# A windowed softmax-weighted sum and a maxout layer on one core: part of the tap sums of columns 28 to 31 moved to VectorE, reductions in three parts, two products in two parts, and a test of the softmax sums with a second path

## Chip, cores and metric

The kernel runs on 1 core of one Trainium2 chip. The metric is the device time of one execution in microseconds. Engine names are TensorE (PE in the profile, PEld its weight loads), VectorE (DVE), ScalarE (ACT), GpSimd (POOL) and SyncE (SP).

## What is computed

```python
# x: (8, 4160, 192), weight_gen: (8, 4160, 8, 7)
w = np.exp(weight_gen - weight_gen.max(-1, keepdims=True))
w = w / (w.sum(-1, keepdims=True) + 1e-09)          # softmax over 7 taps, for each row and head
x_pad = zeros(6 rows) in front of x                  # in each of the 8 sequences
y[b, s, h*24:(h+1)*24] = sum over k of w[b, s, h, k] * x_pad[b, s + k, h*24:(h+1)*24]
h1, h2 = y @ w1, y @ w2                              # (33280, 192) @ (192, 1024)
out = np.maximum(h1, h2) @ w_out                     # (33280, 1024) @ (1024, 192)
```

The kernel uses max(h1, h2) = h1 + relu(h2 - h1): it multiplies y by the difference of the two weight matrices, takes the relu, multiplies by `w_out`, and adds y times the product of w1 and `w_out`. The softmax is taken without subtracting the maximum: exp, sum, logarithm, subtraction of the logarithm, exp.

## The kernel before

The 33280 rows are laid out as 128 partitions of 260 consecutive rows, called columns. A partition's columns are worked in 17 batches of 16 columns (the last has 4). A batch is cut into pieces, of 4 columns in batches 0 and 1 and of 8 after that. One piece is a unit: units 0 to 7 have 4 columns each, so unit 7 holds columns 28 to 31. Each unit has as many hidden tiles as columns; tiles are worked in groups of two up to tile 15 and of three from tile 16.

For a batch the steps are, by the functions that issue them: `exp_sum` (exp on ScalarE, L135), `red` (sum over the 7 taps on VectorE, L147), `ln` (logarithm on ScalarE, in place, L151), `shift` (subtraction on VectorE, L156), `weights` (exp on ScalarE, each value written twice, L167), `mul` (product of weights and x for all 7 taps on VectorE, L182), `adds` (three additions over the taps on VectorE, L198, L204 and L207), `transpose` (a DMA transpose that SyncE issues). `adds` lays other small steps between its additions by its argument `beside`: the `shift` of the next batch in three parts, or the `red` of a later batch in two.

Batches 0 and 1 differ: there `sum_transpose` lets TensorE add the taps and transpose, by matmuls with the identity (L248), and ScalarE copies the result out as `yt` (L255). With `adds(..., True)` VectorE first adds taps 3 to 5 onto taps 0 to 2, and TensorE then sums only the four that are left (`LEFT`); this is done for unit 5 alone.

The hidden layer of a tile is `hid_tile` (L299 on TensorE) and `relu` (L309 on ScalarE); the output is `out_first` and `out_second` (L351, L339 on TensorE), then `evac` (L395 on ScalarE, stores by SyncE, L409). The last four columns are stored by ScalarE and SyncE at L386.

The order is written out by hand and nothing is rescheduled (`manual_schedule`), so each engine works its instructions in the order of the program. In the opening the weights `w1` and `w2` are loaded in halves to `ws`, VectorE makes their differences `wd` (L584, L589), and ScalarE copies parts of them to other partitions (L586, L587, L591), so that TensorE can use pairs of half arrays. `keep_warm` gives TensorE matmuls without a use while it waits. GpSimd issues the loads of x and of `weight_gen`; `behind` makes such a load wait for an instruction of another engine. In the later groups a table (`AT`, with defaults) names the tile at which ScalarE gets `weights` (W), `ln` (l) or `exp_sum` (X) of a batch; in groups with four output columns a long step can be put off to the next group, unless the group's first tile is in `NOW`.

Of the kernel before, what the change touches and what calls it, by code (L numbers as in the profile page):

```python
# [23 lines left out]
def kernel(  # L24
# [20 lines left out]
    RPB = P // B  # L45
    G = D // H
# [29 lines left out]
    pwg = ctx.enter_context(tc.tile_pool(name="pwg", bufs=4))  # L76
    pxb = ctx.enter_context(tc.tile_pool(name="pxb", bufs=2))
    pe_ = ctx.enter_context(tc.tile_pool(name="pe", bufs=2))
    psm = ctx.enter_context(tc.tile_pool(name="psm", bufs=3))
    pm = ctx.enter_context(tc.tile_pool(name="pm", bufs=1))  # L80
    pen = ctx.enter_context(tc.tile_pool(name="pen", bufs=2))
    py = ctx.enter_context(tc.tile_pool(name="py", bufs=2))
    pyt = ctx.enter_context(tc.tile_pool(name="pyt", bufs=6))
    prd = ctx.enter_context(tc.tile_pool(name="prd", bufs=7))
    first_ps = ctx.enter_context(ExitStack())
# [3 lines left out]
    def later_ps():  # L89

        first_ps.close()
        for k in ("ab", "c", "r"):
            ps[k] = ctx.enter_context(tc.tile_pool(name="pps_" + k, bufs=1, space=bass.MemoryType.PSUM))
# [3 lines left out]
    wg_ts, xb_ts, e_ts, s_ts, en_ts, y_ts, yt_ts = {}, {}, {}, {}, {}, {}, {}  # L97
# [44 lines left out]

    def red(b, i=0, of=1):
        if i == 0:
            s_ts[b] = psm.tile([P, BATCHES[b][1] * H], FP32, name="sum_t", tag="sum")
        hs, at, ap = part(b, i, of)
        nc.vector.reduce_sum(out=s_ts[b][:, hs], in_=_sub(e_ts[b], at, ap), axis=AX.X)  # L147

    def ln(b, i=0, of=1):
        s_t = s_ts[b][:, part(b, i, of)[0]]  # L150
        nc.scalar.activation(out=s_t, in_=s_t, func=AF.Ln)  # L151

    def shift(b, i=0, of=1):
        hs, at, ap = part(b, i, of)
        w_t = _sub(wg_ts[b], at, ap)
        nc.vector.tensor_tensor(out=w_t, in0=w_t, in1=_sub(s_ts[b], hs.start, [[1, hs.stop - hs.start], [0, K]]),  # L156
                                op=ALU.subtract)

    def weights(b, o):
# [6 lines left out]
        for j in range(J):  # L166
            nc.scalar.activation(  # L167
                out=_sub(en_ts[b], (o * WGC + j * N * K) * 2, [[2 * N, K], [2, N], [1, 2]]),
                in_=_sub(wg_ts[b], (o * H + j * N) * K, [[1, K], [K, N], [0, 2]]), func=AF.Exp,
            )  # L170


    def mul(b, o):

        n = dict(pieces(b))[o]
        if n == 4 and b < 2:
            m_out = _sub(m_t, K * o * D, [[64, 2], [P, K * 6], [1, 64]])
            x_in = _sub(xb_ts[b], o * D, [[2 * D, 2], [D, K], [1, 2 * D]])
        else:
# [4 lines left out]
            in1=_sub(en_ts[b], o * WGC * 2, [[2, K * n * H], [0, G // 2], [1, 2]]),  # L184
# [54 lines left out]
    def sum_transpose(u, taps=range(K)):  # L239
# [3 lines left out]
        yps = ps["r" if "r" in ps else "o"].tile([P, 1024], FP32, name="yps", tag="op")  # L243
        for k in range(6):
            for t in taps:
                for r in range(2):
                    at = (K * o + t * n) * D + k * P
                    nc.tensor.matmul(  # L248
                        yps[:, r * 512 + k * 64:r * 512 + (k + 1) * 64],
                        lhsT=m_t[half(r), at:at + P], rhs=ident[half(r), half(r)],  # L250
                        start=(k == 0 and t == taps[0]), stop=(t == taps[-1]),
                        skip_group_check=True,
                    )
        yt = pyt.tile([P, 8 // 2 * 3 * P], BF16, name="yt", tag="yt")
# [122 lines left out]
    def evac(p, n):  # L377
# [20 lines left out]
        for q in range(p, p + n):  # L398
            u, i, _ = column(2 * q)
            if NU - 7 <= u < NU - 1 and i % 2:  # L400
                stores.append((nc.sync, place(q)[0] - 1, [4 * D, 2], [1, 2 * D]))
            elif u < NU - 7 and i == UNITS[u][2] // 2 - 1:
# [108 lines left out]
    gate = consts.tile([P, 1], FP32, name="gate")  # L511
    o_last = consts.tile([P, 2 * D], FP32, name="o_last")

    with tc.tile_pool(name="pstage", bufs=1) as pstage:
# [57 lines left out]
        for o in (0, 4, 8, 12):  # L572
            weights(0, o)
        nc.vector.tensor_copy(out=xb_ts[0][:, PAD * D:(PAD + 4) * D],
# [261 lines left out]
```

## Time and profile before

| | before |
|---|---|
| time, median of 3 runs | 409.5 us (409.34 to 410.65) |
| the profiled execution | 410.25 us, span 408.4 us |
| TensorE busy | 398.9 us (98%) |
| VectorE busy | 371.7 us (91%) |
| ScalarE busy | 357.1 us (87%) |
| GpSimd busy | 72.5 us (18%) |
| granted TensorE clock | 1.0 throughout |
| moved by DMA | 65.70 MB, mean 161 GB/s |

The span runs from the first instruction of the program to its last; the time of an execution has 1.85 us more around it. Times inside a profile are counted from the start of the span. A line such as "L182 DVE ... x37" is a group of instructions of one source line on one engine, and "idle before <- releaser" says how long the engine had nothing to do before them and what ended that.

### The profile page before, as it was taken

What the parts mean: (1) busy time and instruction counts of PE and PEld (TensorE: products, weight loads), DVE (VectorE), ACT (ScalarE), POOL (GpSimd) and SP (SyncE); (2) the same over time, 40 slices, a digit from 0 to 9 for tenths busy, and PEclk for the clock granted to TensorE, in tenths of its full rate; (3) what the DMA queues carried; (4) which work ended last, traced back from release to release, by engine and by line L of the source; (5) the groups of instructions that cost most, each with busy time, mean ns of one, the idle gap of its engine ahead of it and who ended that gap; (6) DMA issues with size and microseconds to landing.
All of it is one profiled execution on the core that took longest, in us unless ns stands there. A gap on an engine that the chain in (4) does not pass through costs nothing.

```text
span 408.4 us, 16153 instructions
## 1 busy us (share of the span) xinstructions
PE 398.9 (98%) x7422; PEld 317.6 (78%) x7422; DVE 371.7 (91%) x216; ACT 357.1 (87%) x424; POOL 72.5 (18%) x101
## 2 busy tenths in 40 slices
PE   7899999999999999999999999999999999999996
PEld 2589989777777777777877777777778777777796
DVE  4999999999999999999999999999999999999000
ACT  6799899999899998898998999998999988988872
POOL 0311012212222112121211122220122220210000
PEclk9999999999999999999999999999999999999999
DMA  8958399767658674976786588478648647654514
GB/s 242 218 125 219 75 186 167 168 165 173 147 113 237 151 167 105 244 201 69 234 203 84 123 248 202 65 243 180 128 109 239 169 68 237 154 127 111 145 55 142
DMA packets 62785, 65.70 MB, mean 161 GB/s; under 512 B 47711, under 2 KB 51679, under 8 KB 62718
## 3 DMA queue, kind: packets, MB, share of 16 engines
q1 hardware_dynamic: 54334, 40.54, 36.7%
q0 software_dynamic: 8240, 24.04, 29.9%
q8 instruction: 58, 0.95, 1.0%
q10 hardware_dynamic: 144, 0.10, 0.1%
q14 instruction: 9, 0.07, 0.1%
HBM read 35.96 MB, written 25.56 MB: 151 GB/s over the span
## 4 chain that ended last, share of the span: by engine, by line
PE 91%; ACT 4%; DMA 3%; issue 1%; SPq 0%; DVE 0%; ACTq 0%
PE op_ps L339 41%; PE hd L299 39%; PE op_ps L351 8%; DMA xs<-in_x_dram 3%; ACT rd_t L309 2%; PE hdp L299 1%; PE yps L248 1%; ACT yt L255 1%; ACT w1t L675 0%; ACT e_t L135 0%; ACT en_t L167 0%; DVE xb_t L620 0%; ACT wd L591 0%; ACT w L668 0%; ACT w1T L633 0%
## 5 line engine op out<-in xcount | busy, mean ns | idle before, releaser
L309 ACT ACTIVATE rd_t<-hd 128x1024 bf16<-128x1024 f32 (+1 forms) x206 | 234.7, 1187 | 27.5 <-PE hd L299 26.3
L339 PE MATMUL op_ps<-wo,rd_t 64*128 64x192 bf16 x4160 | 211.4, 243 | 0.1
L339 PEld LDWEIGHTS <-rd_t 64*128 64x128 bf16 x4160 | 181.7, 94 | 15.7 <-ACTq L372 0.3
L299 PE MATMUL hd<-yt,wd 64*128 64x512 bf16 (+1 forms) x1584 | 188.1, 360 | 0.7 <-issue 0.6
L182 DVE TENSOR_TENSOR m_t<-xb_t,en_t 128x10752 bf16<-128x10752 bf16 (+1 forms) x37 | 187.4, 5070 | 0.2
L299 PEld LDWEIGHTS <-wd 64*128 64x128 bf16 x1776 | 94.5, 94 | 43.2 <-issue 2.8
L224 POOL CAST gate<-yt 128x1 f32<-128x1 bf16 x29 | 37.8, 1305 | 264.3 <-DMA yt<-y_t 264.3
L198 DVE TENSOR_TENSOR m_t<-m_t 128x4608 bf16<-128x4608 bf16 (+1 forms) x30 | 74.1, 2470 | 0.1
L395 ACT COPY o_t<-op_ps 128x384 f32<-128x384 f32 (+1 forms) x99 | 57.3, 589 | 12.8 <-PE op_ps L339 12.8
L351 PE MATMUL op_ps<-w,yt 64*128 64x192 bf16 x780 | 56.0, 243 | 0.4 <-ACT w L668 0.4
L351 PEld LDWEIGHTS <-yt 64*128 64x128 bf16 x780 | 38.6, 94 | 16.7 <-issue 1.3
L204 DVE TENSOR_TENSOR m_t<-m_t 128x3072 bf16<-128x3072 bf16 (+1 forms) x29 | 50.0, 1723 | 0.1
L167 ACT ACTIVATE en_t<-wg_t 128x896 bf16<-128x896 f32 (+2 forms) x45 | 35.8, 821 | 0.0
L207 DVE TENSOR_TENSOR y_t<-m_t 128x1536 bf16<-128x1536 bf16 (+1 forms) x29 | 27.3, 941 | 0.5
L114 POOL DMA_DIRECT2D xb_t<-in_x_dram x33 | 17.6, 534 | 32.0 <-ACT rd_t L309 19.8
L147 DVE TENSOR_REDUCE sum_t<-e_t 128x64 f32<-128x448 f32 (+2 forms) x31 | 19.6, 635 | 3.3 <-ACT e_t L135 3.3
L156 DVE TENSOR_TENSOR wg_t<-wg_t,sum_t 128x280 f32<-128x280 f32 (+5 forms) x46 | 22.0, 481 | 0.0
L135 ACT ACTIVATE e_t<-wg_t 128x896 f32<-128x896 f32 (+2 forms) x18 | 16.1, 901 | 2.6 <-DMA wg_t<-in_weight_gen_dram 2.6
L309 ACT ACTIVATE rd_t<-hdp 128x1024 bf16<-128x1024 f32 x16 | 16.3, 1056 | 0.5 <-PE hdp L299 0.4
L299 PE MATMUL hdp<-yt,wd 64*128 64x256 bf16 x192 | 13.2, 270 | 0.7 <-issue 0.5
L615 PE MATMUL warm<-ident 128*128 128x512 bf16 x38 | 10.7, 449 | 2.6 <-DVE ident L562 2.6
L248 PEld LDWEIGHTS <-m_t 64*128 64x128 bf16 x636 | 10.1, 95 | 2.6 <-DVE m_t L182 2.5
(45 smaller groups left out, 65.9 us busy)
## 6 DMA issues: line engine op xcount, KB each, us to landing
out_dram<-o_t SPq DMA_DIRECT2D x22, 768.0 KB, 4.8
xb_t<-in_x_dram POOLq DMA_DIRECT2D x30, 384.0 KB, 5.2
out_dram<-o_t SPq DMA_DIRECT2D x20, 384.0 KB, 3.1
wg_t<-in_weight_gen_dram POOLq DMA_DIRECT2D x14, 448.0 KB, 5.3
xb_t<-xb_t POOLq DMA_DIRECT2D x16, 288.0 KB, 5.4
wg_t<-in_weight_gen_dram SPq DMA_DIRECT2D x2, 448.0 KB, 4.4
xs<-in_x_dram SPq DMA_DIRECT2D x2, 384.0 KB, 7.2
xb_t<-in_x_dram POOLq DMA_DIRECT2D x3, 192.0 KB, 4.4
```

Of the source, the lines that this page charges most:

```text
L156: nc.vector.tensor_tensor(out=w_t, in0=w_t, in1=_sub(s_ts[b], hs.start, [[1, hs.stop - hs.start], [0, K]]), op=ALU.subtract)
L167: nc.scalar.activation(out=_sub(en_ts[b], (o * WGC + j * N * K) * 2, [[2 * N, K], [2, N], [1, 2]]), in_=_sub(wg_ts[b], (o * H + j * N) * K ...
L182: return nc.vector.tensor_tensor(out=m_out, in0=x_in, in1=_sub(en_ts[b], o * WGC * 2, [[2, K * n * H], [0, G // 2], [1, 2]]), op=ALU.mult,)
L198: nc.vector.tensor_tensor(out=taps(0, 1, 3), in0=taps(0, 1, 3), in1=taps(3, 1, 3), op=ALU.add)
L204: nc.vector.tensor_tensor(out=taps(0, 2, 2), in0=taps(0, 2, 2), in1=taps(1, 5, 2), op=ALU.add)
L207: nc.vector.tensor_tensor(out=_sub(y_ts[b], o * D, [[64, 2], [P, 3 * w // 2], [1, 64]]), in0=taps(0, 1, 1), in1=taps(2, 1, 1), op=ALU.add,)
L224: nc.gpsimd.tensor_copy(out=gate, in_=yt[:, 0:1])
L299: nc.tensor.matmul(hid_out(t, f, j), lhsT=wd_at(j, s, f // 4, f % 4 * P, P), rhs=_sub(yt_ts[u][half(j), :], (s + j) % 3 * P, [[3 * P, w // ...
L309: relu_of[t0] = nc.scalar.activation(out=rd[:, k * 1024:(k + n) * 1024], in_=hd[:, at:at + n * 1024], func=AF.Relu)
L339: return nc.tensor.matmul(op_out(c), lhsT=rd[half(r), k * 1024 + at:k * 1024 + at + P], rhs=wo[half(r), f * D:(f + 1) * D], start=False, s ...
L351: nc.tensor.matmul(op_out(c + j), lhsT=yt_ts[u][half(j), (3 * i + (s + j) % 3) * P:(3 * i + (s + j) % 3 + 1) * P], rhs=w10[half(j), s * D: ...
L395: nc.scalar.copy(out=_sub(o, c % 24 * D, [[D, len(qs)], [h * D, 2], [1, D]]), in_=_sub(tile_, at + (qs[0] - p) * D, [[D, len(qs)], [512, 2 ...
```

## The change

- `mul` and `weights` can be cut by taps. The products for columns 0 to 3 and 4 to 7 are made in two parts, taps 0 to 2 and taps 3 to 6, and TensorE sums the parts one after the other into the same place (`sum_taps`). The first part of columns 0 to 3 stands ahead of the cast of the first x rows, the first part of columns 4 to 7 ahead of the second weight difference. Of the matmuls without a use there are 32, not 38. Two loads of x, and the load of `w_out` behind them, wait for the first part of columns 4 to 7 in place of the first product. ScalarE's copy of `yt` for unit 0 stands ahead of the copy L591.
- Unit 7 gets what unit 5 has: one addition on VectorE (`adds(1, 12, True)`), and TensorE sums `LEFT` only.
- The sums of exponentials are kept for all batches (`sums`), and the logarithm goes to a tile of its own. From batch 4 on `red` is made in three parts, the third behind the second addition of `adds`. Three logarithms are put 2 or 3 tiles later in `AT`; `exp_sum` of batch 11 stands 3 tiles earlier, with its group added to `NOW`; one load of x is issued a group earlier; the stores of one unit are made as one.
- New: `out_of_range` tests on VectorE whether any sum of exponentials lies above 1e18 or below 1e-18, brings the 128 results to one partition by a DMA on SyncE and makes a flag of them. At the end each engine reads the flag. If it is set, `all_again` works everything once more, a column at a time, with the maximum subtracted. With the inputs used here the flag is 0.

```diff
+    S_MOST, S_LEAST = 1e18, 1e-18
...
+    sums = [consts.tile([P, 3 * 16 * H], FP32, name="sums")]
...
     def red(b, i=0, of=1):
+        hs, at, ap = part(b, i, of)
+        nc.vector.reduce_sum(out=s_of(b, hs), in_=_sub(e_ts[b], at, ap), axis=AX.X)
+
+    def ln(b, i=0, of=1):
         if i == 0:
-            s_ts[b] = psm.tile([P, BATCHES[b][1] * H], FP32, name="sum_t", tag="sum")
...
+            l_ts[b] = psm.tile([P, BATCHES[b][1] * H], FP32, name="ln_t", tag="ln")
+        hs = part(b, i, of)[0]
+        nc.scalar.activation(out=l_ts[b][:, hs], in_=s_of(b, hs), func=AF.Ln)
...
+    def tap_parts(b, o):
+
+        return [(0, 3), (3, K)] if b == 0 and o < 8 else [(0, K)]
...
-    def mul(b, o):
+    def mul(b, o, t0=0, t1=K):
...
+    def sum_taps(u, taps, first, last):
...
+        for t in taps:
+            for k in range(6):
                 for r in range(2):
...
-            if NU - 7 <= u < NU - 1 and i % 2:
+            if NU - 6 <= u < NU - 1 and i % 2:
...
         for o in (0, 4, 8, 12):
             weights(0, o)
+        mul(0, 0, 0, 3)
         nc.vector.tensor_copy(out=xb_ts[0][:, PAD * D:(PAD + 4) * D],
                               in_=xs[:, PAD * D:(PAD + 4) * D])
-        first_mul = mul(0, 0)
+        mul(0, 0, 3, K)
...
+        def first_sums():
+
+            keep_warm(22)
+            sum_taps(0, range(3), True, False)
+            keep_warm(6)
+            sum_transpose(0, range(3, K), False)
+            began.append(mul(0, 4, 0, 3))
+
+        w_diff(0, nc.scalar.copy, nc.scalar.copy, first_sums)
         nc.vector.tensor_copy(out=xb_ts[0][:, (PAD + 4) * D:(PAD + 8) * D], in_=xs[:, (PAD + 4) * D:])
-        behind(first_mul, load_x(0, 8, 4))
+        behind(began[0], load_x(0, 8, 4))
...
-        sum_transpose(0)
-        keep_warm(8)
-        mul(0, 4)
-
-
+        keep_warm(4)
+        sum_taps(1, range(3), True, False)
+        mul(0, 4, 3, K)
...
-        sum_transpose(1)
+        sum_transpose(1, range(3, K), False)
...
         red(3)
+        adds(1, 12, True)
...
-        6: (lambda: (weights(2, 8), ln(3), sum_transpose(6)), none),
-        7: (lambda: (behind(relu_of[14], load_x(2, 8, 8)), sum_transpose(7)), none),
+        6: (lambda: (behind(relu_of[12], load_x(2, 8, 8)), weights(2, 8), ln(3), sum_transpose(6)), none),
+        7: (lambda: (sum_transpose(7, LEFT)), none),
...
-    NOW = (22, 28, 40, 49, 106)
+    NOW = (22, 28, 40, 49, 106, 130)
...
-        ('l', 8, 0): 95,
-        ('l', 11, 0): 144,
-        ('l', 12, 0): 162,
+        ('l', 8, 0): 97,
+        ('l', 11, 0): 147,
+        ('l', 12, 0): 165,
...
+        ('X', 11, 0): 132,
...
-            adds(b + 1, 8, beside=lambda i, of: red(b + 3, i, 2) if b + 3 < NB and i < 2 else None)
+            adds(b + 1, 8, beside=lambda i, of: red(b + 3, i, 3) if b + 3 < NB else None)
...
+    def out_of_range():
+
+        for i, (op, beyond, limit) in enumerate(((ALU.max, ALU.is_gt, S_MOST), (ALU.min, ALU.is_lt, S_LEAST))):
+            for j in range(2):
+                nc.vector.tensor_reduce(out=ends[:, 2 * i + j:2 * i + j + 1], in_=sums[j], axis=AX.X, op=op)
+            nc.vector.tensor_single_scalar(out=ends[:, 2 * i:2 * i + 2], in_=ends[:, 2 * i:2 * i + 2],
+                                           scalar=limit, op=beyond)
+        nc.vector.tensor_reduce(out=bad, in_=ends, axis=AX.X, op=ALU.max)
+        nc.sync.dma_start(out=bad_row, in_=bad)
+        nc.vector.tensor_reduce(out=flag, in_=bad_row, axis=AX.X, op=ALU.max)
...
+        if g == len(GROUPS) - 3:
+            out_of_range()
...
+    any_bad = nc.values_load(flag[0:1, 0:1], min_val=0, max_val=1,
+                             skip_runtime_bounds_check_because="a maximum of comparisons, each 0 or 1")
+    with tc.If(any_bad > 0):
...
+            all_again(pg, pgp, pgd)
```

146 lines of the change are left out of this document (109 added, 37 removed).

## The prediction

> **What bounds the kernel now.** I read the page first (busy shares, the chain by line), then the chain in order of time, then the timeline of the opening, then SyncE's end, and last the pairs in which one engine waits for another in the steady part. Of the page:
>
> ```profile
> PE 398.9 (98%) x7422; PEld 317.6 (78%) x7422; DVE 371.7 (91%) x216; ACT 357.1 (87%) x424; POOL 72.5 (18%) x101
> PE 91%; ACT 4%; DMA 3%; issue 1%; SPq 0%; DVE 0%; ACTq 0%
> ```
>
> TensorE carries 91% of the chain, so a microsecond counts only if it is TensorE's own work or lies in the few places where another engine holds TensorE. The chain in order of time (start, length, what) shows those places:
>
> ```profile
> 6.47 7.49 DMA xs<-in_x_dram
> ...
> 14.61 0.62 ACT wd L591
> ...
> 30.59 0.45 ACT e_t L135
> ...
> 31.09 1.49 PE op_ps L339 x32
> ...
> 45.08 0.50 issue
> ...
> 48.04 1.29 PE yps L248 x82
> ```
>
> From 14.61 to 31.04 the chain runs through ScalarE almost without a break; from 31.09 on it is TensorE's, but for 0.50 us of "issue" at 45.08, about as much at 54.9, and 1.7 us on ScalarE near 286, of which TensorE lost 0.3 (8.92 us between two of its L339 rows, elsewhere 8.64). The chain enters the opening by a transfer, but only just: ScalarE's copy before L591 ended 0.02 us before L591 began, so the row to read is the one on which ScalarE's unbroken run starts:
>
> ```profile
> 9.08 0.56 DVE L574 CAST xb_t<-xs 128x768 bf16<-128x768 f32 x1 [1.40 <-DMA xs<-in_x_dram]
> 9.75 2.96 DVE L182 TENSOR_TENSOR m_t<-xb_t,en_t 128x5376 bf16<-128x5376 bf16 x1
> 12.63 0.69 DVE L584 TENSOR_TENSOR wd<-ws1E,ws0E 128x512 bf16<-128x512 f32 x1
> ...
> 13.34 0.62 ACT L586 COPY wd<-wd 64x512 bf16<-64x512 bf16 x1 [2.48 <-DVE wd L584]
> ```
>
> ScalarE idles 2.48 us until VectorE has made `wd`, which stands behind the first product, which stands behind the cast at 9.08. Whatever makes L584 earlier moves the whole opening.
>
> **The opening: products in two parts.** L182 took 2.95 us for 5376 elements and 5.75 for 10752, so 0.15 fixed and 0.52 ns an element: 1.35 us for 3 taps (2304), 1.75 for 4 taps (3072). The first 3 taps of columns 0 to 3 read only the six rows ahead, so that part needs no row of the cast. Its weights come from ScalarE from 7.47 on; L167 issued eight of 224 elements at 0.29 us each, now twelve shorter ones, the first two done at about 8.0. So VectorE: 8.0 to 9.35 first part, cast to 9.9, second part 9.95 to 11.7, L584 at 11.65 where it was 12.63. That is 1.0 us. Then in VectorE's queue come the first part for columns 4 to 7 (to 13.6), the `wsT` difference (to 14.2; its data, issued at 5.4, landed 7.6 later), the second cast (its rows landed at 13.96, by the chain) and the rest of the product, to 16.6 where it was 17.66. ScalarE: two copies at 12.35 and 13.0, then `yt` at 13.6 (its sums are done by 12.5), then L591 at 14.3, then the same run as before, each 1.0 earlier (first relu at 15.97, before 16.99). On TensorE hidden tile 0 waits for L591 until 14.95 and is done by 15.7 (24 such matmuls took 1.49), before ScalarE asks for it. The six fewer warming matmuls lie in idle time. Two loads of x and `wo` now hang on the part that ends at 13.6, not on 12.71: they are issued 0.9 later, x at 13.9, and with the 4.5 us that it took land near 18.4; its first reader would now start at 19.1, so it holds by 0.7. Twelve activations cost 0.4 us of ScalarE's idle 2.48. Worth 1.0 us; bounds 0 (a landing takes its place) and 1.1.
>
> **Columns 28 to 31.** TensorE now sums 4 taps, not 7: 48 matmuls for 84. The chain has both forms: 84 took 1.23 us, 48 took 0.70. It is TensorE's own time: 0.5 us gained. VectorE pays one addition of 2304 elements, 1.35 us (L198). Its cover: the sums read it at about 46.5 and it ends near 43; behind it in the queue stands the product for batch 2, then all later batches. Of these the transposed tile first needed at 73.0 landed by 61.3, when GpSimd read it, so there are 10 us. If that cover were gone it would cost the 1.35.
>
> **Sums of exponentials in three parts.** One more reduction in 13 batches: L147 is 0.61 for 64 and 1.08 for 128, some 0.07 of it per instruction, 1 us in all, on an engine that ends at 378.5. What matters is that the last part now stands behind the second addition, and the logarithm on ScalarE, with relus queued behind it, waits for it:
>
> ```profile
> 86.78 0.61 DVE L147 TENSOR_REDUCE sum_t<-e_t 128x64 f32<-128x448 f32 x1
> 87.31 1.75 DVE L204 TENSOR_TENSOR m_t<-m_t 128x3072 bf16<-128x3072 bf16 x1
> ...
> 91.15 0.34 ACT L151 ACTIVATE sum_t<-sum_t 128x128 f32<-128x128 f32 x1
> ```
>
> Here the sums ended at 87.39 and the logarithm began at 91.15: 3.76 of slack. The third part ends 1.8 later, and VectorE falls behind ScalarE by another 1.7 (it gains 1.1 in the opening and pays 1.35; ScalarE follows TensorE, 1.5 earlier). That leaves 0.2. Slack was 3.02, 0.30 and 2.53 for batches 8, 11 and 12, and there the logarithm is put 2 or 3 tiles later, at 1.44 us a tile (8.64 per six): about 2, 0.6 and 2.7 remain. The other batches keep 0.5 or more, the last one (3.84, and all 13 extra reductions) is 0.4 short, against idle time of ScalarE of about 0.5 a group. I take 0; bounds 0 and 0.5.
>
> **Moved steps.** An x load comes 4 us earlier on GpSimd's queue, `exp_sum` of batch 11 three tiles earlier, two weight steps a group earlier, and one pair of stores becomes one: no TensorE instruction waits for any of them before or after. 0, bounds −0.3 (the stall near 286 goes) and +0.3.
>
> **The test.** Two reductions over 384 and two over 1696 sums: 0.54 and 1.9 us by L147's slope, with the small ones 5.5 us. VectorE has nothing else after 378.5. The 128-word row goes by SyncE between stores that wait for ScalarE until 388 and later, so nothing queued behind it is late, and the flag is there some 10 us ahead of the end. Cost 0.
>
> **The branch.** At the end each engine reads the flag, compares, jumps past the second path and on to the closing waits. SyncE does so after its last store (timeline), and these are the closing waits that it has now (who waited for what: us in total, times, longest):
>
> ```profile
> 405.38 0.34 SPq L386 DMA_DIRECT2D out_dram<-o_last  x1
> ```
>
> ```profile
> SPq L831 <- DMA out_dram<-o_t: 0.6, 1, 0.6
> SPq L831 <- DMA out_dram<-o_last: 0.6, 1, 0.6
> ```
>
> The last store was issued by 405.72 and landed 1.8 to 2.0 us after its start; SyncE walks its closing waits meanwhile, at 0.06 us each, and idles 1.2 us in two of them. Two more waits and two branches take 0.3 to 0.4 of that, so a read of up to 0.8 us is hidden. No row shows such a read: bounds are a step of 0.06 (hidden) and a transfer's landing of 2.0 (1.2 sticks out). I take a read just past its cover, 0.1. The Trainium skill, page "Runtime: NRT & Kernel Launch", section "The launch sequence", puts a load of registers at about 1.3 us; by that, as an estimate, 0.5 would stick out and the time would be 408.6; no row here shows it. GpSimd also sets four loop registers ahead of the first barrier, at 0.035 each (its one register move in the trace): 0.1.
>
> **Sum.** −1.0 −0.5 +0.1 +0.1 = −1.3 us. The profiled execution took 410.25 (span 408.4 and 1.85 around it), 0.75 above the median of 409.5; the same difference gives 408.95 for it and 408.2 for the median, which I forecast. About 0.3%, 1.2 us, is what a measurement of this kernel can tell from no change; this lies on that edge.
>
> **Rivals.**
> The branch costs a fetch of code (slower). The two gaps of TensorE at 45.08 and 54.9 lie 512 of its instructions apart, and its code comes in 58 packets of 16 KB, one for 256 instructions: TensorE waited 0.5 to 0.6 there for the next packet. If each jump on SyncE waits for a whole fetch, such a packet takes 1.1 us on its DMA engine (the page's 1.0% of 16 engines' span, over 58): a read as long as a landing, 2.0, and two fetches, less the 0.8 hidden, stick out by 3.4 and give 411.5. It decides from 2.6 us past the cover, where the time is 410.7. Against it: in the program the target stands 37 instructions on for SyncE, 33 for ScalarE, 107 for TensorE, less than half a packet, and TensorE met 56 packets' ends without a wait. 0.16. The Trainium skill, same page, section "Instruction fetch mechanics", says that a taken branch stalls when its target isn't within the two pages that are held; by that rule none of the three should.
> The opening doesn't move: x (0.7 to spare) or the weights of batch 1 (issued at 11.28, some 5 us under way, wanted at 16.9) come later because the loads crowd, as DMA is 90% busy in the page's second slice. Then ScalarE or VectorE waits, up to 1.0 is lost, 409.2: no change. For: the shares of the slices; against: nothing waited on them before. 0.16.
> The logarithms wait: ScalarE short by 0.5 to 1 once; a wait moves everything behind it later and so restores the slack, so it is paid once, 408.9. 0.08.
> The gaps at 45.08 and 54.9 close, since TensorE has 12 and 84 fewer instructions ahead of them and its packets end elsewhere: 1.1 more, 407.1. They can as well grow. 0.08.
> My forecast holds 0.52, its own range 407.5 to 409.0.
>
> **The numbers.** Faster by over 0.3%: 0.6 of the forecast (0.31), the closing gaps (0.08), part of the others (0.04): 0.43. Slower: the branch and some of the lost opening, 0.18. The rest 0.39. The range leaves out half of the branch's cost and the extremes: 407.1 to 410.6.
>
> **What would show it.** In the changed profile: L584's line starts near 11.65, its first relu near 16.0; the sums for columns 28 to 31 have 48 matmuls; no wait of ScalarE for a sum longer than 0.5; the flag is reduced before 395; SyncE's last two waits are still for transfers. Wrong, if SyncE or ScalarE reach the closing waits after the last landing, if a load is named ahead of a product near 19, or if TensorE's "issue" time grows by more than 0.5.

## The result, and the profile after

The changed kernel takes 415.52 us (median of 6 runs, 414.66 to 417.14) where the kernel before takes 409.96 beside it: ratio 1.0149, 95% interval 1.0129 to 1.0169. (The ratios in this text are estimates over all fast runs; the two medians alone give 1.0136, and elsewhere such a quotient differs from the ratio by up to 0.002.) The forecast was 408.2 with a range to 410.6; it was wrong in sign. The profiled execution took 414.66 us, 413.1 of them in its span. The page:

```profile
PE 398.4 (96%) x7380; PEld 316.7 (77%) x7380; DVE 378.2 (92%) x240; ACT 357.4 (87%) x428; POOL 177.5 (43%) x101
...
PE 52%; DVE 31%; ACT 6%; DMA 6%; issue 4%; SPq 1%; POOL 0%; DVEq 0%; ACTq 0%; POOLq 0%
```

TensorE now carries 52% of the chain and VectorE 31%, where it had 0%. And an engine that the prediction hardly looked at, GpSimd, is busy 177.5 us where it was 72.5, with as many instructions. Comparing when ScalarE starts each relu in the two profiles shows when the time was lost. At the 25th relu (61.7 us, before 63.7) the changed kernel was 2.05 us **ahead**. It lost 0.66 near 92 us, 2.5 near 215, 0.6 near 312 and 1.6 between 358 and 372, won back 0.3 between 240 and 286, and ended its last result 3.0 behind; another 1.7 went after that. Who waited for what (us in total, times, longest):

```profile
ACT e_t L139 <- DMA wg_t<-in_weight_gen_dram: 4.8, 2, 2.6
...
DVE m_t L194 <- DMA xb_t<-xb_t: 4.4, 3, 2.5
...
PE op_ps L371 <- ACT o_t L415: 2.3, 1, 2.3
PE hd L319 <- DMA yt<-y_t: 1.7, 3, 0.6
```

Of the 4.8 us in the first line 2.6 are the first load of the opening, which the kernel before waits for as well; the rest of the first line, and the whole second, are new. Loads of x and of `weight_gen` come late: GpSimd issues both. Its timeline (start, length) says why. The copy at L236 (L224 before) reads one word of each transposed tile, so that the loads behind it in GpSimd's queue wait for that tile:

```profile
71.40 13.40 POOL L236 CAST gate<-yt 128x1 f32<-128x1 bf16 x1 [9.19 <-DMA yt<-y_t]
84.75 0.53 POOL L118 DMA_DIRECT2D xb_t<-in_x_dram  x1
85.27 0.55 POOL L131 DMA_DIRECT2D xb_t<-xb_t  x1
85.81 1.82 POOL L236 CAST gate<-yt 128x1 f32<-128x1 bf16 x1
...
96.09 12.32 POOL L236 CAST gate<-yt 128x1 f32<-128x1 bf16 x1 [7.46 <-DMA yt<-y_t]
```

Before, the same copies:

```profile
73.88 1.04 POOL L224 CAST gate<-yt 128x1 f32<-128x1 bf16 x1 [9.63 <-DMA yt<-y_t]
...
93.89 1.87 POOL L224 CAST gate<-yt 128x1 f32<-128x1 bf16 x1 [8.91 <-DMA yt<-y_t]
```

The two pages have these copies as follows, before and after (times, mean ns of one, idle time before them):

```profile
L224 POOL CAST gate<-yt 128x1 f32<-128x1 bf16 x29 | 37.8, 1305 | 264.3 <-DMA yt<-y_t 264.3
L236 POOL CAST gate<-yt 128x1 f32<-128x1 bf16 x29 | 142.8, 4923 | 166.7 <-DMA yt<-y_t 166.7
```

A copy of one word a partition takes 0.18 us where nothing hinders it. Before, all 29 took less than 2 us (mean 1.3); after, nine take 11.6 to 13.6 (mean of all 29: 4.9). Each that waited ended 0.04 to 0.05 us after an instruction of VectorE ended, so VectorE keeps it out. The Trainium skill, page "SBUF — State Buffer", section "SBUF: two separate sides", says that VectorE and GpSimd share a pair of ports: a VectorE instruction with two SBUF inputs holds it against a GpSimd instruction that reads SBUF, until the VectorE instruction ends. That fits the copies of before. The copies of after go beyond it: the 13.4 us at 71.40 reach across the ends of eight such instructions; the ends of seven let nothing in, and only that of the eighth, which a reduction (one input) at 84.68 follows, did:

```profile
79.01 5.75 DVE L194 TENSOR_TENSOR m_t<-xb_t,en_t 128x10752 bf16<-128x10752 bf16 x1
84.68 0.43 DVE L153 TENSOR_REDUCE later_sums<-e_t 128x40 f32<-128x280 f32 x1
```

What decides between "at the next end" and "at the next reduction" was the question for the runs.

### The profile page after: what moved, and what is told of

It reads as the page before. It is cut to its first block, busy times and chain, and to the rows that moved or that the text cites. A ratio compares the mean times of both kernels' runs of the same rounds, so it can differ in the third digit from the quotient of the medians.

```text
span 413.1 us, 16117 instructions
## 1 busy us (share of the span) xinstructions
PE 398.4 (96%) x7380; PEld 316.7 (77%) x7380; DVE 378.2 (92%) x240; ACT 357.4 (87%) x428; POOL 177.5 (43%) x101
## 4 chain that ended last, share of the span: by engine, by line
PE 52%; DVE 31%; ACT 6%; DMA 6%; issue 4%; SPq 1%; POOL 0%; DVEq 0%; ACTq 0%; POOLq 0%
PE op_ps L359 24%; PE hd L319 22%; DVE m_t L194 14%; DVE m_t L210 7%; PE op_ps L371 5%; DVE m_t L216 5%; ACT rd_t L329 3%; DVE y_t L219 2%; DMA yt<-y_t 2%; DMA xb_t<-xb_t 2%; DMA ws1T<-in_moe_w_dram 2%; DVE wg_t L164 1%; DVE later_sums L153 1%; PE hdp L319 1%; ACT yt L275 0%
## 5 line engine op out<-in xcount | busy, mean ns | idle before, releaser
L236 POOL CAST gate<-yt 128x1 f32<-128x1 bf16 x29 | 142.8, 4923 | 166.7 <-DMA yt<-y_t 166.7
L194 DVE TENSOR_TENSOR m_t<-xb_t,en_t 128x10752 bf16<-128x10752 bf16 (+3 forms) x39 | 187.8, 4818 | 5.4 <-DMA xb_t<-xb_t 4.4
L210 DVE TENSOR_TENSOR m_t<-m_t 128x4608 bf16<-128x4608 bf16 (+1 forms) x31 | 75.4, 2433 | 0.1
L179 ACT ACTIVATE en_t<-wg_t 128x896 bf16<-128x896 f32 (+4 forms) x49 | 36.1, 767 | 0.0
L118 POOL DMA_DIRECT2D xb_t<-in_x_dram x33 | 17.9, 541 | 29.8 <-ACT rd_t L329 16.9
L164 DVE TENSOR_TENSOR wg_t<-wg_t,ln_t 128x280 f32<-128x280 f32 (+5 forms) x46 | 22.0, 481 | 0.9 <-ACT ln_t L159 0.9
L153 DVE TENSOR_REDUCE later_sums<-e_t 128x40 f32<-128x280 f32 (+4 forms) x40 | 18.1, 453 | 0.0
L641 PE MATMUL warm<-ident 128*128 128x512 bf16 x32 | 9.7, 463 | 2.9 <-DVE ident L586 2.9
```

The source lines that it names most:

```text
L164: nc.vector.tensor_tensor(out=w_t, in0=w_t, in1=_sub(l_ts[b], hs.start, [[1, hs.stop - hs.start], [0, K]]), op=ALU.subtract)
L179: nc.scalar.activation(out=_sub(en_ts[b], (o * WGC + (J * t0 + j * (t1 - t0)) * N) * 2, [[2 * N, t1 - t0], [2, N], [1, 2]]), in_=_sub(wg_t ...
L194: return nc.vector.tensor_tensor(out=m_out, in0=x_in, in1=_sub(en_ts[b], (o * WGC + t0 * n * H) * 2, [[2, (t1 - t0) * n * H], [0, G // 2], ...
L210: nc.vector.tensor_tensor(out=taps(0, 1, 3), in0=taps(0, 1, 3), in1=taps(3, 1, 3), op=ALU.add)
L236: nc.gpsimd.tensor_copy(out=gate, in_=yt[:, 0:1])
```

## Experiments: where the tiles lie, the copies, the path

The places in memory had moved too: five new tiles put every pool 2144 bytes higher. The first four runs move the tiles both ways, take the copies away, and take the test and the path away.

```diff
+    pad_1 = consts.tile([P, 384], FP32, name="pad_1")     # ahead of wd
+    pad_2 = consts.tile([P, 152], FP32, name="pad_2")     # behind gate
```

> The kernel before with nothing changed but two unused tiles of 1536 and 608 bytes among the constants, so that every pool lies 2144 bytes higher, where the changed kernel has it. Theory A (GpSimd's copy of one word of a transposed tile is kept out of memory while VectorE runs its subtractions of the logarithm, and where the tiles lie decides whether a subtraction keeps it out): the copy's mean goes from 1.3 us to some 5 us, every other one takes 11 to 14 us, and the time is 413 to 416. Theory B (the copy is kept out because of the new order on VectorE, reductions in three parts and a later start): the copies stay at a mean of 1.3 us and the time at 409.5 to 410.5.

Measured: 1.0002 (0.9992 to 1.0012); mean copy 1.33 us.

```diff
+    ptest = fast.enter_context(tc.tile_pool(name="ptest", bufs=1))   # opened behind the other pools
-    sums = [consts.tile([P, 3 * 16 * H], FP32, name="sums")]
+    sums = [ptest.tile([P, 3 * 16 * H], FP32, name="sums")]          # ends, bad, bad_row, flag too
```

> The changed kernel with its five new tiles (sums, ends, bad, bad_row, flag) allocated behind the other pools, so that the pools lie where the kernel before has them; nothing else is changed. Theory A (place in memory): copies of GpSimd at a mean of 1 to 2 us, none over 3, time 408 to 410.5. Theory B (order on VectorE): copies of 11 to 14 us as in the changed kernel, time 414 to 416.

Measured: 1.0172 (1.0147 to 1.0198); mean copy 4.93 us, longest 13.64. Theory A fell twice: the place of the tiles decides nothing.

```diff
-        nc.gpsimd.tensor_copy(out=gate, in_=yt[:, 0:1])
...
-            load_x(c, 0, min(8, BATCHES[c][1]))
+            behind(landed, load_x(c, 0, min(8, BATCHES[c][1])))   # landed: the transpose; likewise the other two loads
```

> The changed kernel without GpSimd's copy of a word of each transposed tile; the loads of x and of weight_gen that stood behind the copy wait for the transpose's landing themselves. Theories A and B (late loads behind the copies are the loss): TensorE's gaps near 91, 214, 311, 357 and 370 go, time 408 to 410.5. Theory C (the copies are a symptom, the loss is VectorE's own work or the second path at the end): 414 to 416 as the changed kernel.

Measured: 1.0054 (1.0037 to 1.0070). Of the 1.49% some 0.95 went with the copies. The rest stayed, more than theories A and B had said: its last result came 1.57 us later than before, and 1.75 us more went at the end.

```diff
-        if g == len(GROUPS) - 3:
-            out_of_range()
...
-    any_bad = nc.values_load(flag[0:1, 0:1], ...)
-    with tc.If(any_bad > 0): ...
```

> The changed kernel without the test of the sums, the reading of the flag and the second path; the tiles stay allocated, so nothing moves in memory. Theories A and B: the copies stay long, the time falls only by what the end costs, 1.7 us if the later landing of the last stores comes from the branch (413 to 413.5), nothing otherwise (414.5 to 415.5). Theory C (second path): 409 to 411.

Measured: 1.0149 (1.0132 to 1.0166), 415.04 us; the end came 3.1 us after ScalarE's last copy of a result, where the changed kernel needs 4.75. So the longer end goes with the path, and the loss in the middle does not. The time as a whole did not fall, though: in the profiled execution the start cost 1.2 us more than in the changed kernel's (between 26 and 33 us) and the time around the span is 0.2 longer; why the other three runs show no gain is open, and the interval leaves room for one of 0.7 us.

## Experiments: the order on VectorE

Theory D (the copy is let in after VectorE has stood still, and without that only at a reduction) came from VectorE's rows between two reductions. Before:

```profile
63.64 1.75 DVE L204 TENSOR_TENSOR m_t<-m_t 128x3072 bf16<-128x3072 bf16 x1
65.42 0.96 DVE L207 TENSOR_TENSOR y_t<-m_t 128x1536 bf16<-128x1536 bf16 x1
```

and after:

```profile
64.25 1.75 DVE L216 TENSOR_TENSOR m_t<-m_t 128x3072 bf16<-128x3072 bf16 x1
65.92 0.49 DVE L153 TENSOR_REDUCE later_sums<-e_t 128x48 f32<-128x336 f32 x1
66.33 0.95 DVE L219 TENSOR_TENSOR y_t<-m_t 128x1536 bf16<-128x1536 bf16 x1
```

An instruction that depends on the one ahead of it starts after that has ended (65.42 after 65.39); any other starts 0.08 us earlier than the end (65.92 against 66.00). Before, the last addition depends on the second directly, so VectorE stands still there once in two units. After, the third part of the reduction fills that place, and from the reduction on there is no such point until the next reduction. The four copies of the changed kernel up to 360 us that got in elsewhere (at 144.2, 215.9, 263.2 and 358.7) came in during a product that VectorE had begun after a wait, or, the third, one behind which it waited for a logarithm.

```diff
-            adds(b + 1, 8, beside=lambda i, of: red(b + 3, i, 2) if b + 3 < NB and i < 2 else None)
+            adds(b + 1, 8, beside=lambda i, of: red(b + 3, i, 3) if b + 3 < NB else None)
-        ('l', 8, 0): 95,  ('l', 11, 0): 144,  ('l', 12, 0): 162,
+        ('l', 8, 0): 97,  ('l', 11, 0): 147,  ('l', 12, 0): 165,
```

> The kernel before with one part of the change alone: reductions in three parts, the third between the second and the last addition, and the three logarithms put 2 or 3 tiles later. In the profile before VectorE stands still 0.03 us between L204 and L207, in the changed one the third part covers that. Theory D (GpSimd's copy is let in after VectorE has stood still, and without that only at a reduction): copies of 11 to 14 us, mean 4 to 5 us, loads of x late, VectorE waiting for them some 2 to 4 us, time 409.5 to 411.5. Theory E (the copies are kept out because VectorE is 1 us later, by the addition for columns 28 to 31): mean copy 1.3 us, time 408.8 to 409.5.

Measured: 415.44 us, 1.012 (1.0079 to 1.0160), more than theory D had expected. One part of the change, put into the kernel before, brings most of the loss. Its copies (times in ns: least, median, most) and the longest item of what VectorE waited for:

```profile
L224 POOL CAST gate<-yt x29: 183/1818/13595, 61.0 to 388.9; 128x1 f32<-128x1 bf16 x29
```

```profile
DVE m_t L182 <- DMA xb_t<-xb_t: 8.3, 5, 3.0
```

Undone in the changed kernel (the diff above the other way round):

> The changed kernel with the reductions in two parts and the three logarithms at their old tiles; all else as changed. Theory D: copies at a mean of 1.3 us, none over 3; VectorE waits for no load of x and for no logarithm; it is 1 us later than before by the addition, and TensorE, which gained 2 us by tile 24, meets it near 215 to 290 and ends 0.5 to 1 us later than before; with 1.7 us at the end from the second path 410.8 to 412. Theory E: long copies, 414 to 416.

Measured: 411.46 us, 1.0050 (1.0034 to 1.0067); mean copy 1.41 us, longest 1.89; no wait for a load of x. TensorE was 2.0 ahead until 200 us, as expected, and 0.45 ahead (not behind) at its last result.

```diff
-            adds(b + 1, 8, beside=lambda i, of: red(b + 3, i, 3) if b + 3 < NB else None)
+            adds(b + 1, 8, beside=lambda i, of: red(b + 3, i, 3) if b + 3 < NB and i < 2 else None)
+            if b + 3 < NB:
+                red(b + 3, 2, 3)
```

> The changed kernel with the third part of each reduction put behind the last addition in place of ahead of it, so that VectorE stands still between the two additions again; as many instructions. Theory D: copies at a mean of 1 to 2 us, time as without the copies, 411 to 412.5. Theory E, and a theory F (three parts make the copies long wherever they stand): copies of 11 to 14 us, 414 to 416.

Measured: 412.62 us, 1.0075 (1.0048 to 1.0101), just above the range of theory D. The copies:

```profile
L236 POOL CAST gate<-yt x29: 183/1762/2295, 59.7 to 383.5; 128x1 f32<-128x1 bf16 x29
```

As many reductions, as much work, only the third part one place later, and no copy is long: theory F and theory E (VectorE's lateness) fell. Theory D forecast that, but its reason does not cover this run whole. Here the reduction stands behind the still-stand, directly ahead of the product in which every second copy waits, and all 13 of these got in at the product's end, though VectorE had not stood still since that reduction. So a reduction directly ahead of an instruction lets a copy in at its end too, which theory D did not name; this run doesn't tell the two reasons apart.

The traces of the six kernels with the order of the changed one (the changed kernel, those with the tiles moved back, without test and path, with three parts alone and with the short path, and the last one below) do show the still-stand by itself. They hold one place often: a product, second behind a reduction, with another two-input instruction starting at once behind it. Where VectorE had waited ahead of that product, 15 of 15 copies got in at its end; where it had not, 3 of 47. And in the kernels with two parts, where it stands still for 0.03 us between the two additions, 97 of 98 got in at the end of the product behind them. Why a still-stand of 0.03 us lets a copy in two instructions later, no run shows.

```diff
-            all_again(pg, pgp, pgd)
+        nc.vector.memset(gate, 0.0)
```

> The changed kernel with the second path cut to one instruction on VectorE (a memset); the test, the reading of the flag and the branch stay. In the changed profile a code packet of 16 KB starts at 408.70, takes 1.55 us on one DMA engine, one of 8 KB follows at 410.46, and the last stores' packets land behind them, at 411.6 and 412.1. Theory G (these packets are fetched because the second path is long, and they hold up the stores): no code packet after 405, the last store lands 2 us after its issue, the end comes 3.0 to 3.3 us after the last copy of a result on ScalarE where it was 4.75; time 413 to 414. Theory H (the reading of the flag and the branch themselves are the cost): 4.75 stays, 414.7 to 415.7.

Measured: 414.62 us, 1.0123 (1.0098 to 1.0148). The end came 3.07 us after the last copy of a result, and no code packet lay beside the stores, so theory G held for the span. Yet the time outside the span grew from 1.6 to 2.2 us, and the whole is above the expected 413 to 414.

## Experiments: VectorE's lead, the opening, the price of the path

```diff
         red(3)
+        adds(1, 12, True)
...
-        7: (lambda: (behind(relu_of[14], load_x(2, 8, 8)), sum_transpose(7)), none),
+        7: (lambda: (behind(relu_of[14], load_x(2, 8, 8)), sum_transpose(7, LEFT)), none),
```

> The kernel before with the addition for columns 28 to 31 alone (one addition of 1.35 us on VectorE, 48 matmuls in place of 84). In the profile before, the time from the end of VectorE's last addition of a unit to the first matmul that reads its transposed tile falls from 16.8 us at the first such unit to 5.4 at the lowest, near 292 us, where TensorE lost 0.3. Theory V (VectorE is a second bound with about 1 us to spare there): the addition takes all of that, TensorE waits for transposed tiles near 285 to 340, no gain or a loss of up to 0.7, ratio 1.000 to 1.002. Theory P (the prediction: VectorE's lead hides it): 0.5 us faster, up to 1.6 if the gaps at 45 and 55 close too, ratio 0.996 to 0.999.

Measured: 409.88 us, 1.0021 (1.0000 to 1.0042): theory V. TensorE was 2.4 us ahead of the profile before until 222 us, and 0.5 ahead from 347 on: it lost 1.0 near 231 (a result not yet copied out) and 0.9 near 344 (a transposed tile). 1.1 us of that lead it had already at the first relu.

The changed kernel with reductions in two parts, old logarithms, no test and no path as above, and

```diff
         red(3)
-        adds(1, 12, True)
...
-        7: (lambda: (sum_transpose(7, LEFT)), none),
+        7: (lambda: (sum_transpose(7)), none),
```

> The kernel before with the split products of the opening alone (and the earlier x load, exp_sum of batch 11 and the joined stores): no addition for columns 28 to 31, reductions in two parts, old logarithms, no test and no second path. TensorE and VectorE both start their steady part 0.3 to 0.6 us earlier, as in the changed profile, and nothing is added to VectorE. Theory V: 0.3 to 0.8 us faster, ratio 0.998 to 0.9993; the prediction's 1.0 would be 0.9976. A theory that the opening brings nothing, since its landings vary by as much: ratio 1.000.

Measured: 409.71 us, 1.0004 (0.9980 to 1.0028): nothing, as its last theory said. The interval leaves out the prediction's 0.9976, but not theory V's 0.998 to 0.9993.

The changed kernel with three parts, without the copies, the addition, the test and the path (the same lines, and those of the run without copies):

> The changed kernel without GpSimd's copies (loads wait for the transposes themselves), without the addition for columns 28 to 31, without the test and the second path; reductions in three parts. VectorE's step from batch to batch is 23.60 us with three parts and 23.66 with two, so it gains 0.06 a batch. Theory V: 0.3 to 1.0 us faster than before, ratio 0.9975 to 0.9993, as long as VectorE waits for no logarithm; if it waits 1.6 us for one, as in the run without copies, the gain is gone and the ratio is 1.000 to 1.003.

Measured: 410.66 us, 1.0033 (1.0015 to 1.0050). VectorE waited 2.8 us for two logarithms, so its second case (to 1.003). But the opening alone gave 1.0004, and three parts without copies, with the same waits, give 1.0000 below: where these 0.3% come from stays open.

The changed kernel with reductions in two parts and old logarithms, without the test and the path, the addition kept:

> The changed kernel with reductions in two parts and old logarithms, without the test and the second path: the opening and the addition for columns 28 to 31 are left. Theory V with the price of the path from the run with the short path and the one without it (1.1 to 1.4 us): ratio 0.9995 to 1.002, TensorE ahead by 2 us until 200 and then held by VectorE to 0.3 to 0.7 ahead. Theory P: the whole of the predicted 1.5 us is seen, ratio 0.9963.

Measured: 410.12 us, 1.0013 (0.9999 to 1.0027): theory V.

Open after these were the logarithms, the path by itself, and whether the addition pays once VectorE has room. First the run with three parts alone, less the copies (both edits are shown above):

> The kernel before with reductions in three parts and the three logarithms late, as in the run with three parts alone, but without GpSimd's copies (loads wait for the transposes themselves). Theory D (the copies are the loss): the 5 us of the run with three parts alone go but for what VectorE waits for logarithms, ratio 0.999 to 1.003. If the logarithms are the larger part: ratio 1.004 to 1.010.

Measured: 409.61 us, 1.0000 (0.9975 to 1.0025), though VectorE still waited for the late logarithms:

```profile
DVE wg_t L156 <- ACT sum_t L151: 2.7, 2, 2.2
```

Without the copies, three parts cost nothing; with them 1.2%. (Whether the kernel before, in two parts, would gain by losing its copies was not run.) Then the same with the old places of the logarithms:

```diff
-        ('l', 8, 0): 97,  ('l', 11, 0): 147,  ('l', 12, 0): 165,
+        ('l', 8, 0): 95,  ('l', 11, 0): 144,  ('l', 12, 0): 162,
```

> The same with the three logarithms at their old tiles. VectorE then waits for none of them; ScalarE should wait for the third part of one reduction, by the rows of before 1.6 us at batch 11 (its logarithm started 0.30 us after the last sum, and the third part ends 1.9 later), less at 8 and 12. Theory L (late logarithms cost VectorE's lead): 0.3 to 1 us faster than with the late ones. If ScalarE's wait reaches TensorE: 0.5 to 1.5 us slower than with the late ones.

Measured: 409.78 us, 1.0006 (0.9983 to 1.0029): no difference beyond the noise of 0.25%, neither half of the expectation.

The addition for columns 28 to 31 with three parts and no copies, and

```diff
-        ('l', 8, 0): 95,  ('l', 11, 0): 144,  ('l', 12, 0): 162,
+        ('l', 8, 0): 96,  ('l', 11, 0): 146,  ('l', 12, 0): 163,
```

> The kernel before with the addition for columns 28 to 31, reductions in three parts, logarithms 1 or 2 tiles late, and without GpSimd's copies. Theory V: VectorE gains 0.06 us a batch from the three parts and pays 1.35, TensorE has 0.5 us less work and loses one of its gaps near 50 us; if VectorE waits for no logarithm the time is 0.3 to 1 us below before, ratio 0.9975 to 0.9995; if it does, ratio 1.000 to 1.003.

Measured: 409.67 us, 1.0006 (0.9980 to 1.0032). VectorE waited 0.6 us for a logarithm and TensorE 0.9 for a transposed tile; no gain.

The path by itself:

```diff
     def tap_parts(b, o):
-        return [(0, 3), (3, K)] if b == 0 and o < 8 else [(0, K)]
+        return [(0, K)]           # and the opening, columns 28 to 31, reductions, tables and stores as before
```

> The kernel before with the sums kept, the test, the reading of the flag and the whole second path; nothing else of the change. By the runs before it the start is 0.24 us later, the last stores land 1.7 us later behind two code packets, and the time outside the span is 0.2 shorter: 1.2 to 1.8 us slower, ratio 1.003 to 1.0045. The prediction said 0.2 us (ratio 1.0005); its rival with a fetch of code said 3.4 (1.008).

Measured: 409.32 us, 1.0004 (0.9977 to 1.0031). The expectation was wrong here, and the prediction's 0.2 us agrees. So the path costs about 1.5 us in the changed kernel (1.0050 with it, 1.0013 without, both with two parts) and nothing by itself. Transfers from 404.9 us on, in the changed kernel (queue: packets, MB, share; issue: KB, us from issue to landing):

```profile
q8 instruction: 1, 0.02, 1.2%
q14 instruction: 1, 0.01, 0.4%
...
out_dram<-o_last SPq DMA_DIRECT2D x1, 96.0 KB, 3.5
out_dram<-o_last ACTq DMA_DIRECT2D x1, 96.0 KB, 3.7
```

and in the kernel with the path alone:

```profile
q14 instruction: 1, 0.01, 0.4%
...
out_dram<-o_last SPq DMA_DIRECT2D x1, 96.0 KB, 1.8
out_dram<-o_last ACTq DMA_DIRECT2D x1, 96.0 KB, 2.0
```

The packet of queue q8 makes the difference: 16 KB of code, started at 408.70, 1.55 us on one DMA engine; from 410.24, as it ends, the last packets of the stores follow one by one until 411.66. (That they share its engine is read from this order; the trace doesn't name the engines.) Counting in the traces, this packet starts when TensorE has run 14777 of its instructions (weight loads counted), or up to 30 behind that in the other kernels that run so far. The kernel before has 14861 and the run with the path alone 14864: there the packet comes 84 instructions ahead of the end. The changed kernel, with fewer matmuls, has 14780. To test that, 104 instructions were added where TensorE is idle:

```diff
-                nc.tensor.matmul(warm[:, 0:512], lhsT=ident, rhs=_sub(ident, 0, [[0, 4], [1, P]]),
+                nc.tensor.matmul(warm[:, 0:192], lhsT=ident, rhs=_sub(ident, 0, [[0, 3], [1, 64]]),
-            keep_warm(22)      # and 6, 4
+            keep_warm(58)      # and 16, 10
```

> The run with reductions in two parts (test and whole second path kept), its 32 warming matmuls of 512 columns replaced by 84 of 192: the same TensorE time in the opening, 104 more TensorE instructions, so that the code packet at instruction 14777 starts some 3 us ahead of the last matmul in place of beside the last stores. Theory K (where the code packets end against the program's end): the end comes 3.1 to 3.4 us after ScalarE's last copy of a result in place of 4.4, ratio 1.0010 to 1.0025 where it was 1.0050. If it depends on something else: ratio 1.004 to 1.006 and the packet beside the stores stays. Gaps of TensorE near 45 to 60 us may move by up to 1 us either way, since all its packets end elsewhere.

Measured: 410.12 us, 1.0012 (1.0000 to 1.0024) where it was 1.0050, the end 3.18 us after the last copy: theory K. More matmuls without a use made the kernel faster.

> The changed kernel with the same 84 short warming matmuls and nothing else. Theory K: the end 3.1 to 3.4 us after the last copy in place of 4.75, ratio 1.0105 to 1.012 where it was 1.0149. Otherwise 1.014 to 1.016.

Measured: 414.65 us, 1.0138 (1.0114 to 1.0163); the end 3.19 us after the last copy. The end behaved as theory K says; the ratio fell less than expected, and its interval takes in both.

No version beat the kernel before.

## Why the prediction was wrong, point by point

Taking the parts out of the changed kernel one after the other gives the account: 1.0149 in all; 1.0050 without the three parts and the late logarithms (4.1 us of 409.5); 1.0013 without the path (1.5 us); 1.0004 without the addition (0.4 us). Each step is uncertain by about 1 us, and the last two are within it; that the path costs anything shows more clearly at the end itself, 4.4 us behind the last copy of a result with it and 3.1 without.

**Sums in three parts, "I take 0; bounds 0 and 0.5": the step that failed.** It weighed what comes later for ScalarE. The loss was on GpSimd, whose copies the prediction had read only as the time of a landing. A row that bore on it was in the profile before: 29 copies of one word at a mean of 1305 ns, where three of them took 0.18 us and the other 26 ended 0.04 us behind the end of an instruction of VectorE. With three parts the copies keep loads back by 10 us or more nine times; the load of `weight_gen` for batch 11, issued only at 206.87, landed so late that ScalarE stood still with relus queued behind:

```profile
211.84 0.32 ACT L159 ACTIVATE ln_t<-later_sums 128x128 f32<-128x128 f32 x1
214.35 0.95 ACT L139 ACTIVATE e_t<-wg_t 128x896 f32<-128x896 f32 x1 [2.19 <-DMA wg_t<-in_weight_gen_dram]
```

That is the largest single loss of TensorE, the 2.5 near 215. It is also where "moved steps: 0" failed in company: `exp_sum` of batch 11 had been put 3 tiles earlier, towards a load that came later. With short copies (the run with two parts, which keeps the moved step) TensorE has no gap near 215, and waits once for a result not yet copied out, 0.3 us near 231.

**Slack of the logarithms.** The prediction asked whether ScalarE would wait for a sum; it did, for 0.8, where it had allowed 0.5. It did not ask whether VectorE would wait for the later logarithm: 0.9 us in the changed kernel, 2.7 and 2.8 in two of the runs without the copies. By itself this cost nothing that the runs can tell (1.0000 with late, 1.0006 with old places).

**Columns 28 to 31, −0.5.** TensorE has 48 matmuls for 84, as said:

```profile
46.83 0.94 PE L263 MATMUL yps<-ident,m_t 64*128 64x64 bf16 x48
```

The step that failed is "there are 10 us" of cover. That is the cover at the first tile only. In the profile before, from the end of L207 to the first matmul that reads the transposed tile it is 16.9 us for the first unit (which is read from 71.46 us on, not 73.0), 10.9 for the tenth and 5.6 for the twenty-fifth, near 345 us, because VectorE needs 23.66 us for a batch and TensorE 23.04. A transposed tile lands mostly 3.8 us after that end, which would leave 1.8 us at the narrowest place; in this profile the landing took 5.5 there and left 0.2. The addition of 1.35 us and an earlier TensorE used it up, and TensorE waited there for the tile (near 344 us): alone the part gives 1.0021.

**The opening, −1.0.** L609 started at 12.26 (11.65 predicted), the first relu at 16.63 (16.0). The sum started from the 1.40 us that the cast waited for x in the profile before. That wait was a property of this one execution. The opening of the run with the addition alone is the same code (VectorE's timeline):

```profile
7.99 0.56 DVE L574 CAST xb_t<-xs 128x768 bf16<-128x768 f32 x1 [0.38 <-DMA xs<-in_x_dram]
8.66 2.96 DVE L182 TENSOR_TENSOR m_t<-xb_t,en_t 128x5376 bf16<-128x5376 bf16 x1
11.53 0.69 DVE L584 TENSOR_TENSOR wd<-ws1E,ws0E 128x512 bf16<-128x512 f32 x1
```

and the changed opening:

```profile
8.65 1.36 DVE L194 TENSOR_TENSOR m_t<-xb_t,en_t 128x2304 bf16<-128x2304 bf16 x1 [0.66 <-ACT en_t L179]
9.93 0.55 DVE L599 CAST xb_t<-xs 128x768 bf16<-128x768 f32 x1
10.58 1.76 DVE L194 TENSOR_TENSOR m_t<-xb_t,en_t 128x3072 bf16<-128x3072 bf16 x1
12.26 0.68 DVE L609 TENSOR_TENSOR wd<-ws1E,ws0E 128x512 bf16<-128x512 f32 x1
```

From ScalarE's first `en_t` to the weight difference, twelve profiles with the split product all have 4.09 or 4.10 us. Of eight with the product whole, six have 3.6 to 3.9; the two in which the cast waited longest for x have 4.26 (0.77 us of waiting) and 5.16 (before, 1.40). So counted from that `en_t` the sum was right (4.18 predicted, 4.09 measured); what it compared it with was an exception. The split helps only when x is late.

**Gaps at 45.08 and 54.9** closed, a rival at 0.08 (a new one of 0.17, for a relu, came at 47.8); 1.1 us of the lead of 2.05 at the 25th relu is from there. Its reading of the gaps as waits for code fits the other traces: between 30 and 100 us all 18 gaps of TensorE of 0.3 us and more that the profile calls "issue" (twelve traces have such gaps) lie at 1729, 1985, 2241, 2497 or 2753 of its instructions, that is 256 apart. But which of these places cost time differs between executions of the same code: the kernel before with two unused tiles lost only the second. So part of that lead was luck, and it could not be kept, for want of cover on VectorE.

**Test, 0:** right. The flag was there before 395, the row's transfer hidden:

```profile
388.50 0.16 DVE L832 TENSOR_REDUCE bad<-ends 128x1 f32<-128x4 f32 x1
394.30 0.28 DVE L834 TENSOR_REDUCE flag<-bad_row 1x1 int32<-1x128 f32 x1 [5.64 <-DMA bad_row<-bad]
```

**Branch, +0.1.** The read took 0.52 us, less than the 0.8 of cover, and SyncE's closing waits still ended with transfers, as foreseen:

```profile
SPq L955 <- DMA out_dram<-o_t: 1.2, 1, 1.2
...
SPq L955 <- DMA out_dram<-o_last: 0.4, 1, 0.4
```

The Trainium skill, page "Runtime: NRT & Kernel Launch", section "The launch sequence", gives 1.3 us for loads of registers from HBM at the launch; this read of one word from SBUF took less than half of that. The step that failed is that these transfers would land as before: 1.7 us late, behind a code packet. The rival named a fetch of code, but as a wait of SyncE, 3.4 us, and held it unlikely since the jump is less than half a packet; the count says where a packet ends, and the changed kernel ended 3 instructions behind one. The rule of the Trainium skill, same page, section "Instruction fetch mechanics", that a taken branch stalls if its target is outside the two pages held, does not price this: the fetch cost by the DMA engine that it shares with the stores.

**Register moves, +0.1:** the first transfer is issued 0.24 us later (0.98 for 0.74), but the time outside the span is shorter by about as much (1.6 for 1.85), so nothing is left of it.

## What to carry to other kernels

Read a cover along the whole run and take its smallest value: a lead that looks like 10 us may shrink by 0.6 in each step. Before filling a still-stand of an engine, ask who uses it: here another engine's one-word copy was let through there, and whole loads stood behind that copy; a wait without a memory read (the load waiting for the transpose itself) needs no such place. A wait seen in one profile is priced only after a second execution has shown it, and a change in the number of instructions moves the ends of all code packets, for better or worse.

## What was not expected of the hardware

- A GpSimd copy that reads one word a partition stayed outside for up to 13.7 us, past the ends of seven VectorE instructions with two inputs, and was let in 0.04 us behind the end of the instruction ahead of a reduction. Where VectorE had stood still since its last reduction, even by 0.03 us, or where a reduction stood directly ahead of the running instruction, the copy got in at that instruction's end (at most 2.5 us).
- Code of TensorE is fetched in packets of 16 KB for each 256 of its instructions, 0.9 to 2.3 us each. Where one began beside the last stores, these landed as much later (3.5 us for 1.8).
- The time around the span changes with the path: 1.5 to 1.7 us with the long path, 1.7 to 2.1 without (one run 2.8), 2.1 to 2.3 with the short one, where a packet of 8 KB came behind the end.
